# Sparse attention with a mixture of experts: the scale bounds of Q and K taken as sums of magnitudes on ScalarE, the two copies of each high half written by one instruction, and four spreads and the first W2 bounds moved by some steps

## The chip, the core and the metric

The kernel runs on one core of one Trainium2 chip. The metric is the device time of one execution in microseconds (us), median of several runs. Engines are named as in the profile: PE (TensorE, matrix products), DVE (VectorE), ACT (ScalarE), POOL (GpSimd), SP (SyncE, which issues nearly all the DMAs).

## What is computed

Attention over 4 batches, 8 heads, 768 positions and a head size of 64, with a block mask (neighbouring blocks, first and last rows and columns of blocks, three sampled blocks a row). Its output, 3072 rows of 512, goes through a softmax gate that is balanced eight times over rows and columns, and then through 8 experts of width 1024, all of them for every row.

```
scores = scale * np.matmul(q, k.transpose(0, 1, 3, 2))
scores = np.where(mask, scores, -1000000000.0)
attn = np.exp(scores - np.max(scores, axis=-1, keepdims=True))
attn = attn / (np.sum(attn, axis=-1, keepdims=True) + 1e-09)
x = np.matmul(attn, v)          # transposed to (batch*seq, heads*dim)
for e in range(E):
    h = np.maximum(x @ w1[e], 0.0)
    out += P[:, e:e + 1] * (h @ w2[e])
```

## The kernel before

All products are made from pairs of 16-bit numbers. A value in 32 bits is scaled by a power of two, its high half is the scaled value rounded to 16 bits, and its low half is what the rounding left. The scale comes from a bound on the magnitudes. That bound is found per partition, spread over the partitions by a transpose on PE (`spread_qk`, L613, for Q and K; `spread_max`, L110, for everything else), reduced on DVE, clamped, and cut to its power of two (`scale_qk`, L619 to L628).

The attention part goes in steps T = 0 to 191, one for each of 32 heads n and each of 6 columns of 128 keys. A step makes four large products of one score tile for the weights (`weights`, L697 and L700), its exponential on ACT (L705), the low half of the exponential on ACT or DVE in turn (`split_lo`, L714 and L716), and three steps later 18 small products with V (`values`, L731). Ten steps ahead of a head its score tiles are made once for their row maxima alone (`scores`, L664 and L667, with the maximum on DVE, L673), which `lower` (L681, L682, and a transposing DMA) folds into Q.

Q and K are loaded for a pair of heads g at a time (`load_qk`, L588). `peak` (L604) takes the largest magnitude of a loaded 128x768 tile on DVE, once for Q and once for K, at steps 12g - 26 and 12g - 24 (for the second pair both at -14). `spread_qk` and `scale_qk` follow at 12g - 20. For each head, `high_qk` writes the high half with two ACT instructions, once to its place (L641) and once to a second place (L642, the "dup"), since the scores need high times high, low times high and high times low. `low_qk` (L646) makes the low half on DVE, and `turn` (L652) has the halves transposed by a DMA.

The order is written out by hand. `at(T, o, fn, ...)` puts a piece of work at a step and a rank within it (FIRST, TURNS, TOPS, SCORES, VALUES, WEIGHTS, LOWS, LATER, LAST); the pieces are then issued by step and rank, and `in_order` keeps each engine in that order. So an instruction that waits holds up all that stands behind it on its engine. Two spare PSUM banks `u` serve in turn, one for the sums of `values` and the other for all spreads and for `turn_x` (L762), which transposes finished heads on PE and copies them out on ACT (`xf`, L769). `turn_x` stands at steps 12j + 6 and 12j + 10. The spreads of V's bounds stand at steps 42, 90 and 138 (and -6 for the first batch), and that of the first W1 at 142.

At the end the experts' stage begins. The first W2 (2 MB, `load_w(2, 0)`, issued at step 184) is bounded by eight maxima on DVE (L187), two at each of the steps 188 to 191, spread (L110) at 193 and turned into a scale at 194. `stage1` (L1167, L1179) makes the first products of the experts, `stage2` (L1282, L1303) the second. From here on the engines' work is queued by a planner with costs and due times (class `Slots`), which the change does not touch.

Of the kernel before, what the change touches and what calls it, by code (L numbers as in the profile page):

```python
# [14 lines left out]
BF16 = mybir.dt.bfloat16  # L15
AF = mybir.ActivationFunctionType
# [10 lines left out]
EXP_SHIFT = 18.664973875118524  # L27
WALL = 2.0 ** 15
QKTOP = 2.0 ** 9
QKTINY, QKHUGE = 1.0, 2.0 ** 50  # L30
HDOWN = 2.0 ** -20
HUP = 2.0 ** 20
EPS = 1e-9
# [22 lines left out]
def tile_sparse_attention_moe(  # L56
# [338 lines left out]
    with ExitStack() as actx:  # L395
# [202 lines left out]
        def peak(g, m):  # L598
            if m == 0:
                qk[g] = tuple(  # L600
                    col.tile([P, w], F32, tag=f"qk{w}{i}", name=f"qk{i}_{g}")
                    for i, w in enumerate((2, 2, 2, 1))
                )
            nc.vector.tensor_reduce(  # L604
                out=qk[g][0][:, m : m + 1],
                in_=raws[g, m].rearrange("p h c d -> p (h c d)"), axis=AX.X,
                op=ALU.max, apply_absolute_value=True,
            )

        def spread_qk(g):  # L610
# [19 lines left out]
        def parts_qk(n, m):  # L630
            g, j = divmod(n, 2)
            t = (qss[n % NQS], kss[n % NKS])[m]
            if m == 0:
                hi, dup, lo = t[:, 0, :, D:], t[:, 1, :, :D], t[:, 0, :, :D]
            else:
                hi, dup, lo = t[:, 0, :, :D], t[:, 0, :, D:], t[:, 1, :, :D]
            return raws[g, m][:, j], qk[g][2][:, m : m + 1], hi, dup, lo

        def high_qk(n, m):
            src, s, hi, dup, _ = parts_qk(n, m)  # L640
            nc.scalar.activation(hi, src, AF.Copy, scale=s)  # L641
            nc.scalar.activation(dup, src, AF.Copy, scale=s)  # L642

        def low_qk(n, m):
            src, s, hi, _, lo = parts_qk(n, m)
            nc.vector.scalar_tensor_tensor(  # L646
                out=lo, in0=src, scalar=s, in1=hi, op0=ALU.mult, op1=ALU.subtract
            )

        def turn(n, m):  # L650
# [162 lines left out]
        for b in range(B):  # L813
            T0 = b * H * NC
            at(T0 - 30 if b else -17, FIRST, load_v, b)
            for n, T in enumerate((-25, -19, -18, -13) if b else (-13, -13, -11, -9)):
                at(T0 + T, LATER, peak_v, b, n)
            at(T0 - 6, TURNS, scale_spread, f"v{b}")
            at(T0 - 12, LATER, room_v, b)
            at(T0 - 6, LATER, scale_v, b)  # L820
# [13 lines left out]
        def start_w():  # L834
            load_w(1, 0)
            parts, whole, spread, power = scale_steps(1, 0)
            for T, part in zip((101, 106, 107, 113, 118, 119, 125, 130), parts):
                at(T, LATER, part)
            at(130, LATER, whole)
            at(142, TURNS, spread)  # L840
            at(142, LATER, power)

        def start_sums():
            one, two, three, by_p = first_sums()
# [13 lines left out]
        def start_w2():  # L858
            load_w(2, 0)
            parts, whole, spread, power = scale_steps(2, 0)  # L860
            for n, part in enumerate(parts):
                at(188 + n // 2, LATER, part)
            at(NTILE, LATER, whole)
            at(NTILE + 1, LAST, spread)
            at(NTILE + 2, LATER, power)

        at(100, FIRST, start_w)
        at(140, FIRST, start_sums)
# [554 lines left out]
```

## Time and profile before

| | us |
|---|---|
| median of 3 runs | 2336.94 (2335.74 to 2338.75) |
| the profiled execution | 2332.6 |
| its span, first to last instruction | 2330.8 |
| attention, first to last exponential (L705) | 37.0 to 454.2 |
| first product of `stage2` (L1282) | 499.0 |
| PE, DVE, ACT, POOL busy | 94%, 86%, 54%, 55% of the span |

The span is what the profiler saw of one execution; 1.8 us of that execution lie around it. A busy share is a mean over the whole span, and the stages differ. In the tables of windows each row is a stretch of the span with the busy time of each engine and, behind it, the granted clock of PE (1.00 is full). In the tables of waits a row says which engine and line stood still for which other engine and line, for how long in total, how often, and the longest.

### The profile page before, as it was taken

The numbers are of one execution on the slowest core, as the hardware profiler recorded it, in microseconds if no ns is written. First come the engines' busy times: TensorE is split into PE (matmuls) and PEld (weight loads), VectorE is DVE, ScalarE is ACT, GpSimd is POOL, SyncE is SP. The second block draws the span as 40 slices with busy tenths as digits, with TensorE's granted clock in tenths as the row PEclk, the third lists the DMA queues.
The fourth block names the chain that finished last, engine by engine and source line by source line (L and its number), as shares of the span: only waits on it lengthen the run. The fifth ranks groups of instructions, "written<-read, shape, count | busy, mean of one in ns | idle before, by whom it ended". The sixth has DMA issues, their size and how long they took to land.

```text
span 2330.8 us, 47300 instructions
## 1 busy us (share of the span) xinstructions
PE 2192.4 (94%) x18892; PEld 1607.8 (69%) x18892; DVE 1999.7 (86%) x3570; ACT 1255.6 (54%) x2173; POOL 1289.9 (55%) x1235
## 2 busy tenths in 40 slices
PE   5999988889899999999999999999999999999999
PEld 3767666657666677677767776777677767776677
DVE  8999999888789888988898889888988898889876
ACT  4888888665465444444444445444444454445442
POOL 2012334496376665756575657565756575657553
PEclk9999999999999999999999999999999999999999
DMA  6667765413112211221122121212121212121221
GB/s 152 131 123 165 188 128 123 136 62 111 48 49 84 85 49 49 84 84 49 57 75 85 48 74 59 85 48 84 49 84 49 84 48 85 49 84 48 76 75 55
DMA packets 191890, 192.36 MB, mean 83 GB/s; under 512 B 131740, under 2 KB 144052, under 8 KB 191668
## 3 DMA queue, kind: packets, MB, share of 16 engines
q1 hardware_dynamic: 191104, 189.30, 28.2%
q8 instruction: 148, 2.42, 0.4%
q14 instruction: 74, 0.61, 0.1%
q10 hardware_dynamic: 564, 0.03, 0.0%
HBM read 140.54 MB, written 17.30 MB: 68 GB/s over the span
## 4 chain that ended last, share of the span: by engine, by line
PE 48%; DVE 8%; POOL 5%; issue 3%; ACT 2%; DMA 2%; DVEq 0%; POOLq 0%; SPq 0%
PE p L1167 24%; PE py L1282 24%; DVE acc L1303 2%; POOL r L1046 2%; DMA r<-in_moe_w_dram 2%; DVE h L1199 1%; POOL h L1199 1%; DVE a L1179 1%; DVE mx_w L187 1%; ACT h L1189 1%; ACT attic L1031 1%; POOL s L1241 1%; DVE u L1179 1%; DVE attic L1035 1%; DVE w2p L1035 1%
## 5 line engine op out<-in xcount | busy, mean ns | idle before, releaser
L1282 PE MATMUL py<-w2p,h 128*128 128x256 f16 x8064 | 952.3, 273 | 19.6 <-DVE w2p L1035 7.8
L1282 PEld LDWEIGHTS <-h 128*128 128x128 f16 x8064 | 790.8, 98 | 159.7 <-issue 19.1
L1303 DVE SCALAR_TENSOR_TENSOR acc<-py,spare,acc 128x256 f32<-128x256 f32 (+1 forms) x840 | 455.1, 579 | 36.4 <-PE py L1282 35.5
L1199 POOL TENSOR_TENSOR h<-u,h 128x384 f16<-128x384 f32 x128 | 126.7, 990 | 589.8 <-ACT h L1189 589.8
L1167 PEld LDWEIGHTS <-attic 128*128 128x128 f16 x3072 | 304.1, 99 | 215.0 <-issue 40.3
L1167 PE MATMUL p<-attic 128*128 128x384 f16 x2304 | 418.5, 331 | 24.6 <-DVE r L1179 19.4
L1167 PE MATMUL p<-arena 128*128 128x384 f16 x2304 | 409.5, 327 | 16.3 <-DVE arena L1035 11.5
L1167 PEld LDWEIGHTS <-arena 128*128 128x128 f16 x2304 | 225.5, 98 | 150.6 <-DVE arena L1035 13.5
L1189 ACT ACTIVATE h<-c 128x384 f16<-128x384 f32 x256 | 133.6, 522 | 342.5 <-DVE c L1179 272.4
L705 ACT ACTIVATE pe<-t,shift,qk 128x768 int32<-128x768 f32 x192 | 189.9, 990 | 73.7 <-PE t L700 67.8
L1179 DVE SCALAR_TENSOR_TENSOR a<-p,a 128x384 f32<-128x384 f32 x384 | 210.8, 549 | 19.8 <-PE p L1167 15.0
L673 DVE TENSOR_REDUCE top<-m 128x1 f32<-128x768 f32 x192 | 181.6, 948 | 12.6 <-PE m L667 12.3
L1189 ACT ACTIVATE h<-r 128x384 f16<-128x384 f32 x256 | 132.4, 521 | 67.5 <-POOL r L1053 63.2
L1241 POOL TENSOR_TENSOR s<-a,u 128x384 f32<-128x384 f32 x128 | 130.9, 1022 | 49.1 <-ACT a L1238 48.9
L1053 POOL TENSOR_TENSOR r<-s,r 128x384 f32<-128x384 f32 x128 | 149.4, 1167 | 10.0
L1053 POOL TENSOR_TENSOR c<-c,r 128x384 f32<-128x384 f32 x128 | 149.3, 1166 | 10.0
L1046 POOL TENSOR_TENSOR r<-r 128x256 f32<-128x256 f32 (+1 forms) x106 | 135.6, 1304 | 26.6 <-DVE arena L1035 26.6
L1167 PE MATMUL p<-arena,attic 128*128 128x384 f16 x768 | 148.4, 330 | 0.0
L1199 POOL TENSOR_TENSOR h<-c,h 128x384 f16<-128x384 f32 x128 | 143.3, 1120 | 3.5 <-ACT h L1189 3.5
L1179 DVE SCALAR_TENSOR_TENSOR r<-p,a 128x384 f32<-128x384 f32 x128 | 70.5, 551 | 83.4 <-PE p L1167 65.9
L664 PE MATMUL m<-kt,qt 128*128 128x512 f16 (+1 forms) x384 | 128.2, 334 | 14.6 <-DVE top L673 7.3
L1189 ACT ACTIVATE h<-s 128x384 f16<-128x384 f32 x128 | 66.9, 522 | 136.5 <-POOL s L1241 136.3
(206 smaller groups left out, 3731.2 us busy)
## 6 DMA issues: line engine op xcount, KB each, us to landing
arena<-xd SPq DMA_DIRECT2D x128, 384.0 KB, 3.9
attic<-xd SPq DMA_DIRECT2D x96, 384.0 KB, 4.1
r<-in_moe_w_dram SPq DMA_DIRECT2D x16, 2048.0 KB, 8.5
arena<-in_q_dram SPq DMA_DIRECT2D x16, 384.0 KB, 4.2
arena<-in_k_dram SPq DMA_DIRECT2D x16, 384.0 KB, 4.6
arena<-in_v_dram SPq DMA_DIRECT2D x4, 1536.0 KB, 7.6
xd<-xs_t SPq DMA_DIRECT2D x16, 384.0 KB, 4.7
out_dram<-acc SPq DMA_DIRECT2D x24, 256.0 KB, 2.0
```

Of the source, the lines that this page charges most:

```text
L664: nc.tensor.matmul(sc[:, lo:hi], lhsT=qt[:, 0, c], rhs=ka[:, lo:hi], start=True, stop=False)
L673: nc.vector.tensor_reduce(out=tops[n][:, c : c + 1], in_=sc[:, :S], axis=AX.X, op=ALU.max)
L705: nc.scalar.activation(pe, sc[:, :S], AF.Exp, bias=shift, scale=qk[n // 2][3])
L1046: lambda c=c: Pinned.gpsimd.tensor_tensor(out=out[:, c], in0=x[:, c], in1=y[:, c], op=op),
L1053: nc.gpsimd.tensor_tensor(out=out, in0=x, in1=y, op=ALU.subtract)
L1167: nc.tensor.matmul(ps, lhsT=w1p[p][:, l, kc, fs], rhs=xp[p][:, r, kc], start=(kc == 0 and m == 0), stop=(kc == KH - 1 and m == 2),)
L1179: nc.vector.scalar_tensor_tensor(out=t, in0=ps, scalar=HDOWN, in1=other, op0=ALU.mult, op1=ALU.add)
L1189: nc.scalar.activation(h[:, 0], src, AF.Relu if relu else AF.Copy)
L1199: eng.tensor_tensor(out=h[:, 1], in0=src, in1=h[:, 0], op=ALU.subtract)
L1241: nc.gpsimd.tensor_tensor(out=s1, in0=a1, in1=u3, op=ALU.add)
L1282: nc.tensor.matmul(py, lhsT=hs[i, p, kc][:, l, tsl], rhs=w2p[p][:, r, kc], start=(kc == 0 and m == 0), stop=(kc == KF // 2 - 1 and m == 2),)
L1303: nc.vector.scalar_tensor_tensor(out=dst, in0=src, scalar=c, in1=dst, op0=ALU.mult, op1=ALU.add)
```

## The change

The bounds of Q and K are no longer the largest magnitude, found on DVE, but the sum of magnitudes along the row, found by one ACT instruction (`AF.Abs` with an accumulated output; its elementwise result goes to a tile `unread` that nothing reads). A sum is at least as large as the maximum, so it is a bound too; the upper clamp is raised. The two copies of a high half are written by one ACT instruction that reads its source twice through a broadcast; for that, Q's high and low halves change places in the tile. Of the work laid out by hand, the spreads of V's bounds and their scales move from 12j + 6 to 12j + 7, the spread and scale of the first W1 from 142 to 143, the eight maxima of the first W2 from 188 to 191 to 192 and 193, their summary from 192 to 194, the spread from 193 to 194 and the scale from 194 to 195.

```diff
@@ -103,6 +103,11 @@
+    unread = const.tile([P, S], BF16, name="unread")
+
+    def magnitude(engine, total, src):
+        engine.activation(unread[:, : src.shape[1]], src, AF.Abs, accum_out=total)
@@ -601,10 +606,9 @@
-            nc.vector.tensor_reduce(
-                out=qk[g][0][:, m : m + 1],
-                in_=raws[g, m].rearrange("p h c d -> p (h c d)"), axis=AX.X,
-                op=ALU.max, apply_absolute_value=True,
+            magnitude(
+                nc.scalar, qk[g][0][:, m : m + 1],
+                raws[g, m].rearrange("p h c d -> p (h c d)"),
             )
@@ -631,20 +635,20 @@
             if m == 0:
-                hi, dup, lo = t[:, 0, :, D:], t[:, 1, :, :D], t[:, 0, :, :D]
+                hi, lo = t[:, :, :, :D], t[:, 0, :, D:]
             else:
-                hi, dup, lo = t[:, 0, :, :D], t[:, 0, :, D:], t[:, 1, :, :D]
+                hi, lo = t[:, 0].rearrange("p c (two d) -> p two c d", two=2), t[:, 1, :, :D]
...
         def high_qk(n, m):
-            src, s, hi, dup, _ = parts_qk(n, m)
+            src, s, hi, _ = parts_qk(n, m)
+            src = src.unsqueeze(1).to_broadcast([P, 2, NC, D])
             nc.scalar.activation(hi, src, AF.Copy, scale=s)
-            nc.scalar.activation(dup, src, AF.Copy, scale=s)
@@ -815,9 +819,9 @@
-            at(T0 - 6, TURNS, scale_spread, f"v{b}")
+            at(T0 - 5, TURNS, scale_spread, f"v{b}")
...
@@ -859,10 +863,10 @@
             for n, part in enumerate(parts):
-                at(188 + n // 2, LATER, part)
+                at(NTILE + n // 4, LATER, part)
```

In the order of the instructions, a name such as `pe_5_730` is the tile, the step within the head, and a running number; the lines of the new kernel lie 4 or 5 further down. First, ACT around step 11 before: two rows for each high half of Q (`qs`) or K (`ks`).

```order
L714 ACTIVATE pl_3_658<-pe_3_656 128x768
L705 ACTIVATE pe_5_730<-t_5_725,shift,qk_0_181 128x768
L641 ACTIVATE qs_110<-arena,qk_2_340 128x6x64
L642 ACTIVATE qs_110<-arena,qk_2_340 128x6x64
L705 ACTIVATE pe_0_765<-t_0_760,shift,qk_1_232 128x768
L714 ACTIVATE pl_5_732<-pe_5_730 128x768
L705 ACTIVATE pe_1_799<-t_1_794,shift,qk_1_232 128x768
L641 ACTIVATE ks_112<-arena,qk_2_340 128x6x64
L642 ACTIVATE ks_112<-arena,qk_2_340 128x6x64
```

The same place in the new kernel:

```order
L718 ACTIVATE pl_3_649<-pe_3_647 128x768
L109 ACTIVATE unread,qk_3_695<-arena 128x768
L709 ACTIVATE pe_5_721<-t_5_716,shift,qk_0_182 128x768
L646 ACTIVATE qs_111<-arena,qk_2_335 128x12x64
L709 ACTIVATE pe_0_755<-t_0_750,shift,qk_1_229 128x768
L718 ACTIVATE pl_5_723<-pe_5_721 128x768
L109 ACTIVATE unread,qk_3_695<-arena 128x768
L709 ACTIVATE pe_1_789<-t_1_784,shift,qk_1_229 128x768
L646 ACTIVATE ks_113<-arena,qk_2_335 128x2x6x64
```

Each pair of rows for a high half is one row of twice the size, and two rows with the sum of magnitudes (L109) stand ahead of two exponentials; the two L604 rows of a pair of heads are gone from DVE. In the whole program ACT has one row that loads a function table, before and now.

Second, DVE at the end of attention before: the low halves (`pl`) of the last steps between the maxima of the first W2 (`mx_w`), then the first combination of the experts' stage (L1179).

```order
L716 TENSOR_SCALAR pl_1_7840<-pe_1_7838 128x768
L187 TENSOR_REDUCE mx_w_0_7730<-r_0_7728 128x1 x2
L716 TENSOR_SCALAR pl_2_7867<-pe_2_7865 128x768
L187 TENSOR_REDUCE mx_w_0_7730<-r_0_7728 128x1 x2
L716 TENSOR_SCALAR pl_3_7901<-pe_3_7899 128x768
L187 TENSOR_REDUCE mx_w_0_7730<-r_0_7728 128x1 x2
L716 TENSOR_SCALAR pl_4_7934<-pe_4_7932 128x768
L187 TENSOR_REDUCE mx_w_0_7730<-r_0_7728 128x1 x2
L716 TENSOR_SCALAR pl_5_7963<-pe_5_7961 128x768
L1179 SCALAR_TENSOR_TENSOR r_0_0_8130<-p_0_0_8131,a_0_0_8121 128x384
```

The same place in the new kernel:

```order
L720 TENSOR_SCALAR pl_1_7777<-pe_1_7775 128x768
L720 TENSOR_SCALAR pl_2_7804<-pe_2_7802 128x768
L720 TENSOR_SCALAR pl_3_7836<-pe_3_7834 128x768
L720 TENSOR_SCALAR pl_4_7867<-pe_4_7865 128x768
L720 TENSOR_SCALAR pl_5_7894<-pe_5_7892 128x768
L192 TENSOR_REDUCE mx_w_0_7667<-r_0_7665 128x1 x8
L1183 SCALAR_TENSOR_TENSOR r_0_0_8067<-p_0_0_8068,a_0_0_8058 128x384
```

All eight maxima now stand behind the last low half and still ahead of the first combination.

Third, PE around step 42 before: the transposes of a finished head (`xn`), with the spread of V's bound right behind them.

```order
L731 MATMUL u_144<-attic,pe_2_1779 128x66
L762 MATMUL u_145<-ident,xn_2_1556 128x128 x3
L110 MATMUL u_145<-ident,mx_v_1207 128x128
L664 LDWEIGHTS qt_100
L664 MATMUL m_4_1915<-kt_104,qt_100 128x512
```

The spread in the new kernel, one step further:

```order
L735 LDWEIGHTS pe_3_1797
L735 MATMUL u_145<-attic,pe_3_1797 128x66
L115 MATMUL u_146<-ident,mx_v_1193 128x128
L668 LDWEIGHTS qt_101
L668 MATMUL m_5_1928<-kt_105,qt_101 128x512
```

Between `xn` and the spread, which share a bank, there now lies a whole step of products. POOL and SP keep their order.

More of the change, by code (lines that the diff above doesn't have):

```diff
@@ L29 @@
 QKTOP = 2.0 ** 9
-QKTINY, QKHUGE = 1.0, 2.0 ** 50
+QKTINY, QKHUGE = 1.0, 2.0 ** 60
 HDOWN = 2.0 ** -20
@@ L817, in tile_sparse_attention_moe @@
                 at(T0 + T, LATER, peak_v, b, n)
-            at(T0 - 6, TURNS, scale_spread, f"v{b}")
+            at(T0 - 5, TURNS, scale_spread, f"v{b}")
             at(T0 - 12, LATER, room_v, b)
-            at(T0 - 6, LATER, scale_v, b)
+            at(T0 - 5, LATER, scale_v, b)
             for h, hi, lo in ((0, -4, -2), (2, 3, 5), (4, 8, 10), (6, 15, 17)):
@@ L839, in start_w @@
             at(130, LATER, whole)
-            at(142, TURNS, spread)
-            at(142, LATER, power)
+            at(143, TURNS, spread)
+            at(143, LATER, power)
         def start_sums():
@@ L861, in start_w2 @@
             for n, part in enumerate(parts):
-                at(188 + n // 2, LATER, part)
-            at(NTILE, LATER, whole)
-            at(NTILE + 1, LAST, spread)
-            at(NTILE + 2, LATER, power)
+                at(NTILE + n // 4, LATER, part)
+            at(NTILE + 2, LATER, whole)
+            at(NTILE + 2, LAST, spread)
+            at(NTILE + 3, LATER, power)
         at(100, FIRST, start_w)
```

6 lines of the change are left out of this document (3 added, 3 removed).

## The prediction

> **What bounds the kernel now.** First the page, then the busy time of each engine by stretches of the span. Columns: stretch, its length, busy time of PE, PE's weight loads, DVE, ACT, POOL, then PE's granted clock.
>
> ```profile
> 0.00:30.00 30.00, 9.66 (x43) 4.97 (x44) 24.85 (x66) 8.53 (x16) 6.99 (x25) 1.00 0.70 185
> 30.00:90.00 60.00, 55.42 (x648) 36.96 (x648) 55.85 (x106) 43.06 (x57) 8.56 (x13) 0.91 0.66 136
> 90.00:150.00 60.00, 56.92 (x769) 41.02 (x768) 56.83 (x118) 49.22 (x68) 5.64 (x6) 1.00 0.61 114
> 150.00:210.00 60.00, 59.73 (x842) 43.29 (x839) 58.20 (x108) 54.81 (x75) 11.30 (x15) 1.00 0.71 156
> 210.00:270.00 60.00, 53.84 (x729) 38.19 (x726) 54.87 (x100) 48.09 (x66) 21.16 (x25) 0.97 0.70 164
> 270.00:330.00 60.00, 57.22 (x806) 41.35 (x804) 58.94 (x113) 50.74 (x68) 16.56 (x21) 1.00 0.73 154
> 330.00:390.00 60.00, 50.26 (x658) 35.41 (x658) 56.62 (x103) 47.66 (x65) 27.95 (x27) 1.00 0.62 125
> 390.00:450.00 60.00, 51.79 (x791) 38.11 (x789) 54.46 (x76) 50.41 (x64) 30.96 (x26) 1.00 0.61 167
> 510.00:2331.00 1821.00, 1747.11 (x13273) 1296.66 (x13272) 1531.05 (x2708) 868.43 (x1632) 1119.83 (x1045) 0.99 0.20 67
> ```
>
> From 510 us on PE is busy for 1747 of 1821 us, and no instruction there is touched. In attention two engines are nearly full at once: DVE has 91 to 98% of each stretch, PE 84 to 99.6%, and ACT, at 72 to 91%, is third. Which of them sets the pace changes: between 150 and 210 us PE stands still for 0.27 us, between 330 and 390 for 9.74 us.
>
> Then the waits between 30 and 390 us, the stretch in which most of the bounds are taken, and one row of them from 210 to 270 us (the last one).
>
> ```profile
> DVE top L673 <- PE m L667: 9.3, 10, 2.0
> PE u L110 <- ACT xf L769: 7.7, 4, 2.5
> PE m L664 <- DVE top L673: 7.0, 7, 2.2
> PE t L697 <- DVE top L673: 6.2, 9, 2.8
> DVE mx_w L187 <- DMA r<-in_moe_w_dram: 3.0, 1, 3.0
> PE u L613 <- DVE xn L752: 2.1, 4, 0.7
> PE u L762 <- DVE xn L752: 1.8, 2, 1.0
> PE t L697 <- DVE top L673: 3.0, 2, 2.8
> ```
>
> PE waits for DVE for 7.0 + 6.2 + 2.1 + 1.8 = 17.1 us. The longest of these, 2.8 us, lies behind the one wait of DVE for a load (`mx_w`), which stays; 14.3 us are left. A further 7.7 us PE waits in a spread (L110) for ACT to empty the bank (`xf`).
>
> **Part by part: the bounds leave DVE.** By groups, between 30 and 390 us, first the group of DVE and then groups of ACT:
>
> ```profile
> L604 DVE TENSOR_REDUCE qk<-arena 128x1 f32<-128x768 f32 x28 | 26.3, 939 | 0.0
> L705 ACT ACTIVATE pe<-t,shift,qk 128x768 int32<-128x768 f32 x162 | 160.3, 990 | 59.9 <-PE t L700 54.3
> L641 ACT ACTIVATE qs<-arena,qk 128x384 f16<-128x384 f32 x27 | 16.3, 604 | 1.0 <-DVE qk L626 1.0
> L284 ACT ACTIVATE xs_b<-xf 128x768 f16<-128x768 f32 x10 | 8.3, 832 | 0.0
> ```
>
> DVE loses 28 of the 32 maxima here, of 939 ns each, 26.3 us or 4.4 us in 60; the other four lie before 30 us. The end of the stretch can gain from that only what PE waits for DVE, so 14.3 us is the upper end. The lower end is 0: ACT becomes late in DVE's stead. I take 9 us, about 60%, because PE itself is the next to be late. It is busy for 59.73 of 60 us in one stretch, where the 4.4 us bring nothing, and DVE in turn waits 9.3 us for PE, so a part of what DVE gains it waits away.
>
> ACT takes on 28 sums. No instruction of before accumulates on ACT. Without that, one over 128x768 takes 832 ns (L284) or 990 ns (L705, with operands for scale and bias); if the accumulator were read in a second pass it would be twice the latter, 1.98 us. I take 0.9 us, near the two rows: 25 us.
>
> The merged copies go the other way. Two of 604 ns become one of twice the size. From 384 elements (604) and the same with 768 (832 without, 990 with two operands), I take 0.92 us for it, and the bounds are 0.83 and 2 x 0.604 = 1.21. There are four such groups of 27 (Q and K, first and second copy; one is shown), so 54 pairs: 54 x (1.21 - 0.92) = 15.7 us less. So ACT goes from 293.6 us (the sum of its six rows) to about 303 of then some 345 us, 88%. That is below the 91% which it has between 150 and 210 us, and the extra work is hidden behind the exponentials' own waits for PE (54.3 us). If that cover is gone, each sum costs its 0.9 us. A sum stands four steps or more ahead of the spread that needs it, about 8 us at 2.2 us a step, which is the 417 us of this row over 191 steps:
>
> ```profile
> L705 ACT ACTIVATE pe<-t,shift,qk x192: 976/992/997, 37.0 to 454.2; 128x768 int32<-128x768 f32 x192
> ```
>
> So no engine waits for a sum, save at the start.
>
> **The spreads a step later.** The four waits of 7.7 us are, by their place behind `xn`, the V spreads of three batches and the first W1. Each stands right behind `xn` in the same bank, so that PE holds all products until ACT has come round to `xf`. One step of about 2 us, with its products, now lies between; of waits of at most 2.5 us half a microsecond is left at most. I take 5 us, since only what PE's standstill passes on to DVE (`top` waiting for `m`, 9.3 us) is lost to both; the ends are 0 and 7.7. V's scale comes a step later, and POOL, which makes the high halves at 12j + 8, may start on them later. `values` uses them at 12j + 15, eight steps or some 17 us behind the scale; W1's scale has four steps to its first use at 147. So I set the delay at nothing, and at its own step (2 us) if that cover is gone.
>
> **The start.** Operations of before at the start (start and length in us):
>
> ```profile
> 4.37 1.28 ACT L641 ACT_TABLE_LOAD   x1 [4.37 <-DMA arena<-in_q_dram]
> 6.66 1.80 DVE L604 TENSOR_REDUCE qk<-arena 128x1 f32<-128x768 f32 x2
> 9.04 0.42 DVE L621 TENSOR_REDUCE qk<-u 128x2 f32<-128x256 f32 x1 [0.57 <-PE u L613]
> ```
>
> DVE came to the first two maxima only at 6.66, behind the mask's work, and ended them at 8.46. ACT is free when its table is in, at 5.65, and ends two sums of 0.9 us at 7.45: 1.0 us earlier, for all that follows. The ends are a loss of 1.1 us (two sums of 1.98 us would end at 9.61) and a gain of 1.2 (two of 0.83).
>
> **The end of attention.** DVE, ACT and, in the last two rows, all engines in two stretches:
>
> ```profile
> 446.53 0.55 DVE L716 TENSOR_SCALAR pl<-pe 128x768 f16<-128x768 uint16 x1
> 450.34 1.28 DVE L187 TENSOR_REDUCE mx_w<-r 128x1 f32<-128x512 f32 x2 [3.26 <-DMA r<-in_moe_w_dram]
> 451.53 0.55 DVE L716 TENSOR_SCALAR pl<-pe 128x768 f16<-128x768 uint16 x1
> ...
> 456.50 0.55 DVE L716 TENSOR_SCALAR pl<-pe 128x768 f16<-128x768 uint16 x1
> 458.60 0.56 DVE L1179 SCALAR_TENSOR_TENSOR r<-p,a 128x384 f32<-128x384 f32 x1 [1.55 <-ACT a L1214]
> ...
> 459.51 0.56 DVE L1179 SCALAR_TENSOR_TENSOR a<-p,a 128x384 f32<-128x384 f32 x1 [0.29 <-PE p L1167]
> 460.49 0.56 DVE L1179 SCALAR_TENSOR_TENSOR u<-p,a 128x384 f32<-128x384 f32 x1 [0.42 <-PE p L1167]
> ```
> ```profile
> 448.54 0.99 ACT L705 ACTIVATE pe<-t,shift,qk 128x768 int32<-128x768 f32 x1 [0.25 <-PE t L700]
> 454.20 0.99 ACT L705 ACTIVATE pe<-t,shift,qk 128x768 int32<-128x768 f32 x1 [4.67 <-PE t L700]
> ```
> ```profile
> 450.00:454.00 4.00, 1.86 (x15) 1.17 (x16) 3.66 (x7) 0.00 (x0) 0.00 (x0) 0.58 0.14 56
> 454.00:458.00 4.00, 4.00 (x38) 2.73 (x37) 3.05 (x6) 1.45 (x2) 0.00 (x0) 0.57 0.02 4
> ```
>
> DVE waits 3.26 us for the W2 load with finished exponentials behind it. The low half that PE needs comes at 451.53, so PE is idle for half of four microseconds, then runs at a granted clock of 0.57, and ACT waits 4.67 us for the last score tile. In the new order the low halves go ahead: the next at about 447.0, the last exponential at 449.5 (right behind the one of 448.54) and its low half by 451.5. Then the eight maxima, 8 x 0.64 = 5.1 us, to 456.6; the load is there by then (450.34). The first combination starts at 456.6 in place of 458.60. In the next two combinations DVE waited 0.29 + 0.42 = 0.7 us for PE; now PE makes their products while the maxima run. That gives 2.0 + 0.7 = 2.7 us. The W2 scale moves with it and is used only by the splitting of W2, whose first product (`stage2`) starts at 499.0 in the table above; the products of `stage1` up to there cover it. The spread of W2 now stands on PE ahead of the last `xn`, which comes later by that one small transpose.
>
> The lower end is 0, if POOL's sums or the late parts of x take it back. For the upper end, PE has 1.86 + 4.00 = 5.9 us of work in the eight microseconds at a granted clock of 0.575; at full clock 2.5 us less, so 2.7 + 2.5 = 5.2 us. The Trainium skill, "TensorE: Matmul & The Clock Gate", section "Part 1: The HAM clock gate", says that the clock halves after an idle window of some 3.4 us and comes back only after as long a busy one. The trace agrees in kind: the clock is still at 0.57 in the second row, where PE is busy throughout. By that rule, with PE's standstill gone, the term would be the 5.2 and the sum 20.2 in place of 17.7. I keep 2.7, because in the new order the maxima on DVE end last and not PE.
>
> **The sum.** 1.0 + 9 + 5 + 2.7 = 17.7 us. The profiled execution, 2332.6 us with 1.8 outside the span, would be at about 2315; the median of before lies 4.3 above that execution, at 2336.94, and I take the same difference off it: **2319 us**.
>
> **The rivals.**
> *All of PE's waits go.* DVE no longer paces attention at all, and PE runs through: 1.2 + 14.3 + 7.7 + 5.2 = 28.4 us, 2308.5. For it: more DVE work goes (26.3 us) than PE waits (14.3). Against it: the stretches where PE is already full, and the ones from 390 us on, in which no bound is taken. Chance 0.15.
>
> *ScalarE holds up what DVE gives free.* A sum stands directly ahead of two exponentials in twelve steps, and these come 0.9 us later; low halves and `values` follow them. Then the 9 us are 0, the spreads give half and the end 2: 1 + 0 + 2.5 + 2 = 5.5, 2331. For it: ACT at 91% in the densest stretch. Against it: three steps between an exponential and its use. Chance 0.15.
>
> *Slower: the function table is swapped.* If the sum of magnitudes needs another table than the exponential, ACT loads one before and one after each sum. The trace has one load in all:
>
> ```profile
> L641 ACT ACT_TABLE_LOAD  x1: 1283/1283/1283, 4.4 to 4.4; - x1
> ```
>
> 28 x 2 x 1.28 = 72 us more: ACT would have 303 + 72 = 375 us of work for a stretch of 360. At the 97% that DVE reaches at most over 60 us (58.20), the stretch takes 387 us, 27 more than now, and with some 4 us back at start and end the time is 2336.9 + 27 - 4 = 2360. It decides from where ACT has 0.97 x 360 = 349 us of work: 46 us over the 303, or 1.6 us more for each sum. A very dear accumulator would come to the same. Against it: exponential and copy share a table now, and the written order has one load, as before. By the Trainium skill, "ScalarE: Activation LUTs", section "Table sets: the hidden batching unit", the magnitude function lies in the set of the exponential, as a filler of every set, so no swap would come. The same page, "What ACT_TABLE_LOAD costs", gives about 2.66 us for a swap with its drain, twice the price used here; no run here shows either. Chance 0.04.
>
> **Chances and range.** The forecast has 0.62 (gains of 11 to 25 us), the first two rivals 0.15 each, the third 0.04; 0.04 is for none of these. A range of 2308 to 2331.5 takes in the first two, and with them the upper ends of all four terms; what it leaves out is the third, the unnamed, and the case in which every term is at its lower end (no gain), about one in eight in all. A measurement of this kernel tells a difference of about 0.2%, 4.7 us, from none. Faster by more than that: 0.62 + 0.15 + two thirds of 0.15 = 0.87; within: the rest of that and some of the unnamed, 0.08; slower: 0.05.
>
> **What would show it.** Right: DVE's 26 us of bounds gone, sums on ACT near 0.9 us and merged copies near 0.92; no wait of L110's spread for `xf` beyond half a microsecond; PE's waits for `top` between 30 and 390 us down by about 60%; no wait of DVE for the W2 load, the first L1179 about 17 us earlier than 458.6, and the stage from there to the end as long as before. Wrong: more than one table load; sums above 2 us; new waits of PE for `pe`; or the first product of `stage2` less than 10 us earlier.

## The result, and the profile after

| | before | after | the same changed kernel, timed again (e7) |
|---|---|---|---|
| median, us | 2337.85 (first set), 2336.21 (e7's set) | 2311.48 | 2315.81 |
| ratio to before, 95% interval | | 0.9892 [0.9868, 0.9917] | 0.9916 [0.9903, 0.9930] |
| profiled execution, us | 2332.6 | 2309.9 | 2319.4 |
| its span, us | 2330.8 | 2308.1 | 2317.5 |
| first exponential | 37.0 | 34.7 | 34.7 |
| exponential of step 180 | 432.1 | 418.6 | 421.1 |
| first product of `stage2` | 499.0 | 483.6 | 484.0 |
| from there to the end of the span | 1831.8 | 1824.5 | 1833.5 |

The change makes the kernel faster, by 25.2 us in the first set (19.4 to 30.8, from the interval times 2337.85) and by 19.6 in the second (16.4 to 22.7). Both hold together between 19.4 and 22.7, so about 20 us is the figure to explain. By the profiles, 15.4 and 15.0 us of it lie ahead of the first product of `stage2`. The 7.3 us by which the stage behind it is shorter in the first profile are not the change's: in e7, the very same program, that stage takes 1.7 us more than before. Over the profiles of all kernels here it takes 1824.5 to 1834.2 us, and none of them changes an instruction there. (What the clock has to do with that spread is in the last section.)

First the busy time by stretches in the changed kernel, columns as in the prediction: stretch, length, PE, weight loads, DVE, ACT, POOL, granted clock.

```profile
30.00:90.00 60.00, 58.16 (x694) 39.24 (x694) 54.09 (x106) 49.12 (x63) 7.82 (x13) 0.91 0.65 139
90.00:150.00 60.00, 59.13 (x804) 42.81 (x803) 55.62 (x116) 53.10 (x69) 5.63 (x6) 1.00 0.63 125
150.00:210.00 60.00, 58.94 (x846) 42.71 (x845) 53.70 (x100) 55.78 (x75) 12.27 (x17) 1.00 0.68 149
210.00:270.00 60.00, 55.96 (x736) 40.15 (x734) 55.26 (x104) 51.63 (x68) 24.15 (x24) 0.97 0.78 173
...
330.00:390.00 60.00, 53.07 (x728) 37.85 (x726) 57.78 (x97) 51.51 (x68) 29.33 (x27) 1.00 0.54 120
```

PE is fuller: 58.16 of 60 us between 30 and 90 (55.42 before), 59.13 between 90 and 150 (56.92). DVE is down by 1.2 to 4.5 us in the first three rows, and ACT reaches 55.78 of 60. A stretch holds more steps than before, so a row is not the same work; the next two are, from the first exponential to that of step 180, first of before, then of after.

```profile
37.00:432.10 395.10, 366.54 (x4975) 261.74 (x4975) 374.65 (x687) 328.72 (x439) 106.23 (x114) 0.99 0.66 142
```
```profile
34.70:418.60 383.90, 364.81 (x4974) 261.58 (x4974) 356.60 (x660) 338.95 (x436) 107.40 (x116) 0.99 0.67 146
```

The same 4974 or 4975 products take PE 365 to 367 us in both. What shrinks is the time in which PE stands still, from 395.10 - 366.54 = 28.6 us to 19.1. DVE is relieved of 18.1 us, and ACT has 10.2 us more.

These are PE's and DVE's waits in the changed kernel between 30 and 380 us, about the steps that 30 to 390 held before (engine, line and what it waits for: total, times, longest).

```profile
DVE top L677 <- PE m L671: 15.9, 25, 1.7
PE t L701 <- DVE top L677: 11.2, 13, 2.4
PE m L668 <- DVE top L677: 3.1, 3, 1.9
DVE mx_w L192 <- DMA r<-in_moe_w_dram: 3.0, 1, 3.0
PE u L766 <- DVE xn L756: 2.5, 4, 0.8
```

The spreads' wait for `xf`, 7.7 us before, is gone. PE's waits for `top` are not: 14.3 us here, 13.2 before. The waits that did fall are those for `xn` (2.5 us; 3.9 before). DVE in turn waits 15.9 us for PE, where it waited 9.3.

Most of the waits for `top` stand behind work of DVE that the change leaves alone, which goes some way to explain why they stay. From the first exponential to step 180 PE waits 13.6 us for `top` in the kernel before. Only 2.5 us of that come where a maximum of Q or K started on DVE within the 4.5 us (two steps) ahead of the late `top`; with 6 us it is 4.1. The rest follows `lower`, the low halves of V, the scale chains of Q and K, and the maxima of W1. Of the 3.9 us of waits for `xn`, 1.9 have such a maximum within 4.5 us. One late `top` behind `lower` (L682, now L686), with the product that waits for it, before and then after:

```profile
423.21 1.20 DVE L682 SCALAR_TENSOR_TENSOR qs<-top,qs 128x6 f16<-128x6 f32 x1
424.31 0.94 DVE L673 TENSOR_REDUCE top<-m 128x1 f32<-128x768 f32 x1
...
425.31 0.38 PE L697 MATMUL t<-qt,kt 128*128 128x512 f16 x1 [1.70 <-DVE top L673]
```
```profile
409.73 1.20 DVE L686 SCALAR_TENSOR_TENSOR qs<-top,qs 128x6 f16<-128x6 f32 x1
410.83 0.94 DVE L677 TENSOR_REDUCE top<-m 128x1 f32<-128x768 f32 x1
...
411.82 0.38 PE L701 MATMUL t<-qt,kt 128*128 128x512 f16 x1 [1.69 <-DVE top L677]
```

What the changed instructions cost, by line (duration in ns, least, median and most; first and last start):

```profile
L109 ACT ACTIVATE unread<-arena x32: 827/836/842, 4.4 to 366.7; 128x768 bf16<-128x768 f32 x32
L109 ACT ACTIVATION_READ_ACCUMULATOR unread<-arena x32: 185/192/199, 5.1 to 367.4; 128x1 f32 x32
L109 ACT ACT_TABLE_LOAD  x1: 1283/1283/1283, 2.0 to 2.0; - x1
```
```profile
L646 ACT ACTIVATE qs<-arena,qk x32: 922/927/937, 9.0 to 390.7; 128x768 f16<-128x768 f32 x32
```

A sum is two instructions, 836 and 192 ns, and overlaps itself a little: at the start the pair begins at 4.39 and ends at 5.32, 0.93 us, against the 0.9 assumed. A merged copy takes 0.927 us (0.92 assumed). There is one table load in the whole program, now ahead of the first sum.

The start of the changed kernel (start and length, in us):

```profile
2.03 1.28 ACT L109 ACT_TABLE_LOAD   x1 [2.03 <-issue]
4.39 0.84 ACT L109 ACTIVATE unread<-arena 128x768 bf16<-128x768 f32 x1 [1.08 <-DMA arena<-in_q_dram]
5.14 0.18 ACT L109 ACTIVATION_READ_ACCUMULATOR unread<-arena 128x1 f32 x1
7.16 0.42 DVE L625 TENSOR_REDUCE qk<-u 128x2 f32<-128x256 f32 x1 [0.41 <-PE u L617]
```

The table is loaded while Q is still on its way, so the first sum starts with Q's landing, at 4.39, and the reduction that stood at 9.04 stands at 7.16.

At the end of attention, two views: ACT's last exponential, and DVE.

```profile
437.38 0.99 ACT L709 ACTIVATE pe<-t,shift,qk 128x768 int32<-128x768 f32 x1 [0.21 <-PE t L704]
```
```profile
438.41 0.56 DVE L720 TENSOR_SCALAR pl<-pe 128x768 f16<-128x768 uint16 x1 [0.64 <-ACT pe L709]
438.88 4.83 DVE L192 TENSOR_REDUCE mx_w<-r 128x1 f32<-128x512 f32 x8
443.63 0.55 DVE L1183 SCALAR_TENSOR_TENSOR r<-p,a 128x384 f32<-128x384 f32 x1
```

The last exponential waits 0.21 us for its tile, not 4.67. The eight maxima of W2 follow the last low half without a wait for the load, and the first combination follows them at once, at 443.63 (458.60 before).

### The profile page after: what moved, and what is told of

The parts are those of the page before. It is cut to its first block, busy times and chain, and to the rows that moved or that the text cites. A ratio compares the mean times of both kernels' runs of the same rounds, so it can differ in the third digit from the quotient of the medians.

```text
span 2308.1 us, 47281 instructions
## 1 busy us (share of the span) xinstructions
PE 2178.5 (94%) x18892; PEld 1602.8 (69%) x18892; DVE 1980.7 (86%) x3538; ACT 1269.1 (55%) x2173; POOL 1287.1 (56%) x1235
## 4 chain that ended last, share of the span: by engine, by line
PE 49%; DVE 8%; POOL 5%; issue 3%; ACT 2%; DMA 2%; DVEq 0%; POOLq 0%; SPq 0%
PE py L1286 25%; PE p L1171 25%; DMA r<-in_moe_w_dram 2%; DVE acc L1307 2%; POOL r L1050 2%; DVE h L1203 1%; POOL h L1203 1%; DVE a L1183 1%; ACT h L1193 1%; DVE mx_w L192 1%; ACT attic L1035 1%; POOL r L1057 1%; DVE w2p L1039 1%; POOL a L1057 1%; POOL s L1245 1%
## 5 line engine op out<-in xcount | busy, mean ns | idle before, releaser
L1171 PE MATMUL p<-attic 128*128 128x384 f16 x2304 | 411.1, 327 | 27.8 <-DVE r L1183 19.2
L1183 DVE SCALAR_TENSOR_TENSOR a<-p,a 128x384 f32<-128x384 f32 x384 | 211.2, 550 | 18.9 <-PE p L1171 13.6
L1203 DVE TENSOR_TENSOR h<-s,h 128x384 f16<-128x384 f32 x128 | 110.1, 860 | 37.2 <-ACT h L1193 37.0
L701 PE MATMUL t<-qt,kt 128*128 128x512 f16 (+1 forms) x384 | 127.0, 331 | 14.0 <-DVE top L677 13.8
```

The lines of the kernel that those rows point to most:

```text
L701: nc.tensor.matmul(sc[:, lo:hi], lhsT=kt[:, 0, c], rhs=qa[:, lo:hi], start=True, stop=False)
L1171: nc.tensor.matmul(ps, lhsT=w1p[p][:, l, kc, fs], rhs=xp[p][:, r, kc], start=(kc == 0 and m == 0), stop=(kc == KH - 1 and m == 2),)
L1183: nc.vector.scalar_tensor_tensor(out=t, in0=ps, scalar=HDOWN, in1=other, op0=ALU.mult, op1=ALU.add)
L1203: eng.tensor_tensor(out=h[:, 1], in0=src, in1=h[:, 0], op=ALU.subtract)
```

## The experiments

Each part of the change was put into the kernel before by itself, then in pairs and triples. A is the sums on ACT, B the merged copies, C the spreads a step later, D the W2 bounds at the end of attention. Times are medians; each ratio is to the kernel before on the same chip.

| | us | ratio, 95% interval | difference, us | first exponential to step 180 | first product of `stage2` |
|---|---|---|---|---|---|
| before (profile of the page) | 2336.94 | | | 395.1 | 499.0 |
| A (e1) | 2326.80 | 0.9967 [0.9955, 0.9979] | -7.7 | 393.5 | 495.4 |
| B (e2) | 2333.30 | 0.9994 [0.9984, 1.0005] | -1.4 | 396.3 | 500.2 |
| C (e3) | 2327.59 | 0.9976 [0.9962, 0.9989] | -5.6 | 391.9 | 495.7 |
| D (e4) | 2331.64 | 0.9986 [0.9975, 0.9998] | -3.3 | 399.9 | 502.3 |
| A, C (e9) | 2323.68 | 0.9946 [0.9934, 0.9959] | -12.6 | 386.5 | 488.3 |
| B, C, D (e5) | 2323.61 | 0.9947 [0.9932, 0.9961] | -12.4 | 392.4 | 492.7 |
| A, C, D (e10) | 2318.56 | 0.9921 [0.9906, 0.9936] | -18.5 | 386.3 | 484.0 |
| all (e7) | 2315.81 | 0.9916 [0.9903, 0.9930] | -19.6 | 386.4 | 484.0 |

The four single differences add up to 18.0 us, and the whole has 19.6: in time, the parts add up, within these intervals. One profile of attention can be off by some us, as D's row shows: that kernel is faster by its times and 3.3 us later at `stage2` in its one profile. The mean granted clock from the first exponential to step 180 also differs among the profiles, from 0.978 (e11) and 0.981 (D) to 1.000 (e12); by estimate 0.01 of some 385 us is about 4 us. Where the two differ, the times decide.

**A alone: the sums (e1).** The upper clamp is raised too.

```diff
...
+    unread = const.tile([P, S], BF16, name="unread")
+    def magnitude(engine, total, src):
+        engine.activation(unread[:, : src.shape[1]], src, AF.Abs, accum_out=total)
...
-            nc.vector.tensor_reduce(
...
+            magnitude(
```

> Only the bounds move from DVE to ACT; two copies, all spreads and the W2 maxima as before. Measure: start of the first product of stage2 (499.0 us before, 483.6 with the whole change), and the length from there to the end (1831.8 and 1824.5). If DVE's freed time is what attention gains from: first product of stage2 at 488 to 492 (1 to 2.3 us at the start, 6 to 9 us behind it). If ACT's queue holds it up without the merged copies: 496 or later. The rest of the span: if the 7.3 us there come from PE's clock and differ by run, anything from 1824 to 1833; if the new tile shifts addresses and so speeds the experts' stage, near 1824.5.

Measured: 7.7 us faster. The profile has 3.6 of them ahead of `stage2`, 2.3 at the start and 1.3 behind it, and none later; the rest is not located, since that profiled run, 2329.8, lay 3.0 above the kernel's own median, and that of before 4.3 below. Here are the waits of this kernel between 30 and 386 us:

```profile
DVE top L677 <- PE m L671: 21.4, 24, 2.5
PE t L701 <- DVE top L677: 9.9, 13, 1.8
PE u L115 <- ACT xf L773: 7.1, 4, 1.8
PE m L668 <- DVE top L677: 3.9, 3, 2.2
...
PE u L766 <- DVE xn L756: 0.7, 1, 0.7
```

DVE's gain shows as DVE's own waiting, 21.4 us for PE. PE waits as long for `top` as before (13.8 us), and the spreads hold it up as before (7.1). What fell is PE's wait for `xn`, to 0.7 us from 3.9. The first product of `stage2`, at 495.4, came later than the 488 to 492 that I had put it at, and just short of the 496 of the other case. So DVE's relief brings less in the steps than forecast (7.7 us less the start's 2.3 is 5.4, against 9), and not by the waits that were to give it.

**C alone, and A with C (e3, e9).** e3 moves these three places and no other; e9 is e1 and e3 together.

```diff
-            at(T0 - 6, TURNS, scale_spread, f"v{b}")
+            at(T0 - 5, TURNS, scale_spread, f"v{b}")
...
-            at(T0 - 6, LATER, scale_v, b)
+            at(T0 - 5, LATER, scale_v, b)
...
-            at(142, TURNS, spread)
-            at(142, LATER, power)
+            at(143, TURNS, spread)
+            at(143, LATER, power)
```

> Only the spreads of V and of the first W1 move by a step. Theory: PE's four waits of 7.7 us for the bank go, and 3 to 5 us of them reach the end of attention: first product of stage2 at 494 to 496. Rival, DVE paces those steps alone: waits gone, but 498 to 499.5.

> Only the sums on ACT and the moved spreads of V and W1; two copies, and the W2 maxima as before. If the parts add up: exponential of step 180 at 424 to 425 (3.9 + 3.8 us). If they help each other, because the freed time is waited away at the spreads when these stay: 419 to 421. Time: 0.57% below before if additive, 0.75% or more if not.

Measured: C gains 5.6 us, A and C together 12.6, about their sum of 13.3. Step 180 of e9 came at 421.3, where it was put if the two help each other (419 to 421), but the time of 0.54% is that of parts that add. PE's waits from the first exponential to step 180, first of C alone (36.4 to 428.3 us), then of A with C (34.8 to 421.3 us):

```profile
PE t L697 <- DVE top L673: 9.6, 11, 2.5
PE u L762 <- DVE xn L752: 3.4, 4, 1.0
PE u L613 <- DVE xn L752: 2.9, 4, 1.2
...
PE m L664 <- DVE top L673: 2.2, 5, 0.6
...
PE u L110 <- ACT xf L769: 0.6, 1, 0.6
```
```profile
PE t L701 <- DVE top L677: 13.2, 16, 1.8
PE u L766 <- DVE xn L756: 2.3, 3, 0.8
...
PE m L668 <- DVE top L677: 1.1, 2, 0.9
```

With C the wait for `xf` goes from 7.7 to 0.6, and the next late thing is `xn` on DVE: 3.4 + 2.9 = 6.3 us, where the kernel before had 3.9. With the maxima off DVE, that falls to 2.3. The waits for `top` do not fall, both rows together grow from 11.8 to 14.3. So the sums pay where PE waits for the finished head, and not at the row maxima.

**B alone, and all but B (e2, e10).** In e2 only the high halves are merged; e10 is the changed kernel with the two separate copies of before.

```diff
...
 def high_qk(n, m):
-            src, s, hi, dup, _ = parts_qk(n, m)
+            src, s, hi, _ = parts_qk(n, m)
+            src = src.unsqueeze(1).to_broadcast([P, 2, NC, D])
             nc.scalar.activation(hi, src, AF.Copy, scale=s)
-            nc.scalar.activation(dup, src, AF.Copy, scale=s)
```

> Only the two copies of a high half become one instruction. If ACT has slack: first product of stage2 at 498 to 499.5, no change of time (within 3 us). If ACT is late in attention and its 15 us of relief count: 496 or earlier, 3 us or more faster.

> The whole change but for the merged copies: each high half is again written by two instructions (some 18 us more on ACT, 64 x 0.28). The sums made twice had cost 15 us of time for 33 us on ACT. If ACT stands at the margin once it makes the sums: exponential of step 180 at 424 to 430 us (418.6 and 421.1 in two profiles of the whole change), time 4 to 10 us above the whole change. If the copies bring here what they bring alone (0.06%): step 180 at 422 or earlier, time within 3 us.

Measured: B alone is not told from nothing (the interval holds 1). Taken out of the whole, no cost can be told either: 0.9921 and 0.9916 have intervals that overlap nearly whole. ACT's busy time from the first exponential to step 180 is 346.42 us of 386.30 in e10, 90%, against 338.95 of 383.90:

```profile
34.70:421.00 386.30, 363.86 (x4974) 260.78 (x4974) 357.77 (x660) 346.42 (x493) 107.56 (x116) 0.99 0.66 145
```

The merged copies' 7.5 us are room on ACT from which no gain can be told here.

**D alone (e4).**

```diff
-                at(188 + n // 2, LATER, part)
-            at(NTILE, LATER, whole)
-            at(NTILE + 1, LAST, spread)
-            at(NTILE + 2, LATER, power)
+                at(NTILE + n // 4, LATER, part)
+            at(NTILE + 2, LATER, whole)
+            at(NTILE + 2, LAST, spread)
+            at(NTILE + 3, LATER, power)
```

> Only the maxima, spread and scale of the first W2 move. Theory: last low half and first combination come 2.5 to 4.5 us earlier and it stays so: first product of stage2 at 494.5 to 496.5. Rival, POOL's sums or the late parts of x take it back: first combination earlier, but first product of stage2 at 498 or later.

Measured: 3.3 us faster, the interval from 0.5 to 5.8. The profile's first product of `stage2` is late, at 502.3, because that execution had lost time in attention, ahead of anything that D touches. From the exponential of step 186 to that product it takes 52.8 us, where before took 56.2, A alone 56.6 and C alone 56.8. The kernels with D have 51.8 to 53.0 there, those without it 54.5 to 56.8. So D gives about 3 us.

**All but A (e5).** The changed kernel with the maximum on DVE kept, and its old upper clamp.

```diff
-            magnitude(
...
+            nc.vector.tensor_reduce(
...
+                op=ALU.max, apply_absolute_value=True,
```

> The whole change but for the sums: bounds of Q and K stay maxima on DVE. Measure in the profile: exponential of step 180 (432.1 us before, 418.6 with the whole change, 428.2 with the sums alone, 428.3 with the spreads alone). If the parts add up: 428, and a time about 8 us above the whole change (the sums alone gave 0.33%). If the sums are worth more once the spreads no longer hold PE: 428 too, but 10 us or more above the whole change; so it is the next kernel, sums and spreads alone, that tells the two apart together with this one.

Measured: 12.4 us faster than before, so the sums are worth 12.4 to 19.6, that is 7.2 us, with the rest in place. The two single profiles have more, 392.4 - 386.4 = 6.0 us up to step 180 and 1.7 at the start. Alone A had 7.7 by its times: the two agree.

**The changed kernel unaltered (e7)** was run beside these.

> The changed kernel once more, unaltered, for more runs of it. If the 7.3 us that the experts' stage was shorter in its first profile come from a chance of that run: the part from the first product of stage2 on takes 1824 to 1833 us here, and the median is 2312 to 2320. If they belong to the kernel: 1824 to 1826, median 2309 to 2313.

Its numbers stand in the tables above: the gain is there again, and the short experts' stage of the first profile is not.

**Each sum twice, and no sum at all (e6, e11).** If ACT's work were what holds up the changed kernel, twice the sums would cost, and none would gain.

```diff
     def magnitude(engine, total, src):
         engine.activation(unread[:, : src.shape[1]], src, AF.Abs, accum_out=total)
+        engine.activation(unread[:, : src.shape[1]], src, AF.Abs, accum_out=total)
```

> The whole change with each sum of magnitudes made twice on ACT: 32 more of about 1.0 us (an elementwise pass of 0.84 and the read of the accumulator, 0.19). The output is the same. If ACT has the slack that the prediction gave it: exponential of step 180 within 3 us of 418.6, start 1 to 2 us later, time within 4 us of the whole change. If ACT is the next to be late: step 180 later by 8 to 30 us.

e11 leaves out the finding of the bounds: a fixed 300.0 stands in their place.

```diff
+        level = aconst.tile([P, 2], F32, name="level")
+        nc.vector.memset(level, 300.0)
...
-            magnitude(
...
+                qk[g] = (level,) + qk[g][1:]
```

> The whole change with no bound found at all: Q and K take a fixed one (300, near the sums of these data), and ACT makes no sums; spreads and scales stay. What it leaves out is the finding of the bounds. If ACT's 33 us of sums cost time at the rate at which doubling them did: step 180 at 403 to 413, time 8 to 16 us below the whole change. If PE and the PSUM buffers are next to be late: within 4 us of the whole change.

Measured: e6 2331.11 us, 0.9980 [0.9971, 0.9989], 15.3 us above e7. e11 2310.84, 0.9900 [0.9885, 0.9916]: by the ratios 3.7 us below all of the change, with intervals that overlap. That is less than the 8 to 16 us which e6's rate would give, and not told from none. In attention its profile gains nothing, with the first product of `stage2` at 485.1 (484.0 in e7), but its granted clock there is 0.978 against 0.986 in e7, which by estimate hides some 3 us. The stretch from the first exponential to step 180, of e6 and of e11:

```profile
35.50:436.40 400.90, 369.40 (x4976) 261.55 (x4976) 359.64 (x660) 362.07 (x491) 109.80 (x116) 0.99 0.64 140
```
```profile
34.70:421.50 386.80, 367.36 (x4976) 263.18 (x4976) 356.39 (x659) 321.99 (x383) 106.75 (x116) 0.98 0.67 145
```

ACT does 322 us in e11, 339 in the changed kernel, 346 in e10, and the stretch stays at 384 to 387 us. At 362, in e6, it is 400.9. The sums, then, cost a few us on ACT at most, with room for some 7.5 us more and not for 23. And new waits appear in e6 (35.5 to 436.4 us):

```profile
DVE pl L721 <- ACT pe L710: 11.2, 13, 1.7
PE u L736 <- ACT pl L719: 4.6, 10, 0.7
```

DVE waits 11.2 us for exponentials and PE 4.6 for low halves of ACT; between 30 and 386 us the changed kernel has 0.4 of the first. The rival in which ScalarE holds up what DVE gives free is real, one more 0.9 us for each sum away. Whether it is ACT's total or the block of 2 us straight ahead of an exponential, these runs don't tell.

**The next wait (e8).** In the changed kernel DVE waits 3.0 us for the first W1 load. This kernel is the changed one with the first maximum over that load four steps later.

```diff
-            for T, part in zip((101, 106, 107, 113, 118, 119, 125, 130), parts):
+            for T, part in zip((105, 106, 107, 113, 118, 119, 125, 130), parts):
```

> The whole change with the first of the eight maxima of the first W1 moved from step 101 to step 105, so that DVE does not stand for its load (3.0 us, with PE idle and its clock halved behind it). If that standstill reaches the end: steps 102 to 108 take about 13 us in place of 17.7, and the time is 3 to 5 us below the whole change. If DVE makes it up elsewhere: within 2 us.

Measured: 2310.65 us, 0.9896 [0.9882, 0.9911]. The two rows are that maximum, in e7 and in e8:

```profile
245.85 0.69 DVE L192 TENSOR_REDUCE mx_w<-r 128x1 f32<-128x512 f32 x1 [3.07 <-DMA r<-in_moe_w_dram]
```
```profile
250.62 0.68 DVE L192 TENSOR_REDUCE mx_w<-r 128x1 f32<-128x512 f32 x1
```

The wait is gone, the steps 96 to 108 take 26.1 us (29.5 after, 30.9 in e7), those from 102 on 13.7 of them (about 13 expected), and the first product of `stage2` comes at 478.0. By the times the gain on e7 is 0.9916 against 0.9896, some 5 us; the intervals touch, so it is likely and not proven. At the same mean granted clock of 0.990 e8 took 2309.7 and 2310.1 us, e7 2315.5 to 2319.4, on different chips. It is the earliest `stage2` of all kernels here.

**DVE loaded again (e12).** e8, with a third of the low halves on ACT in place of a half, the others on DVE.

```diff
-PLAN = 'da'
+PLAN = 'dda'
```

> As the kernel with the first W1 maximum moved, and in addition ACT makes a third of the low halves of the exponentials up to step 178 and not half of them: some 29 fewer of 0.83 us on ACT, as many more of 0.59 us on DVE. If ACT is the late engine after the change: 4 to 10 us below the kernel with the moved maximum alone. If DVE is then late in its stead: within 3 us of it, or slower.

Measured: 2323.22 us, 0.9948 [0.9935, 0.9961], 12.6 us slower than e8. The stretch from the first exponential to step 180:

```profile
34.40:424.40 390.00, 363.11 (x4975) 260.66 (x4975) 374.27 (x690) 319.38 (x407) 109.73 (x116) 1.00 0.66 144
```

DVE is back at 374.27 us, as busy as in the kernel before (374.65). ACT has the least to do of all, and it does not help. So DVE's load still decides in the changed kernel, though PE's waits for `top` never moved much (15.3 us here, 13.7 in e8; those for `xn` are 4.5 and 2.5).

## Why the prediction was right, and where its reasons were not

Forecast 2319 us, 17.7 us below the median before; measured 2311.48 and 2315.81, or 19.6 to 25.2 us less. Both times lie in the range. Point by point:

- **The start, 1.0 us forecast, 2.3 measured.** The term was mis-sized in one assumption: that the table load stays behind Q's arrival, to 5.65 us. In the changed kernel it waits for nothing and is in by 3.31. The first sum starts at 4.39, when Q has landed. By the reduction (9.04 to 7.16) that gives 1.9 us; where the other 0.4 up to the first exponential come from is not located.
- **The bounds off DVE, 9 us forecast with part of it at 60% of PE's waits.** Measured -7.7 alone and -7.2 with the rest, the start's 2.3 (1.7 against e5) in it, so 5.4 or 5.5 us in the steps: between the ends 0 and 14.3, below the value taken. The failed step is "PE's waits for `top` between 30 and 390 us down by about 60%". They stayed (13.2 and 14.3 us), and few of them stood close behind a maximum of Q or K: 2.5 of 13.6 us, and 1.9 of 3.9 for `xn`, 4.4 together. That is the likely reason, read from the order of DVE's rows; no run moved the other work, and in C, where 1.5 of the 6.3 us for `xn` have such a maximum close ahead, 4.0 fell. The relief itself was mis-sized as well. Only 18.1 us went from DVE's busy time, because neighbouring rows of DVE overlap: the 27 maxima of this stretch are 25.4 us long by their rows, but by the trace DVE's busy time without them would be only some 21 us less. In C against A with C, what fell was PE's wait for `xn`, 6.3 to 2.3, and DVE's own wait for PE, 10.5 us up to step 180 before, is 16.9 to 22.6 in the kernels with A, save e12 (9.1). The step priced the relief by the waits with the largest totals, without asking what DVE did ahead of each.
- **ACT takes the sums without cost.** Right to within some 4 us: without any sum (e11) no gain is told from none. The margin was too wide. The prediction let ACT become late from 1.6 us more for each sum, and e6 loses 15.3 us to about 0.9 us more for each; e10 bounds the margin from the other side.
- **Merged copies, nothing forecast.** Right: -1.4 us alone, not told from 0, and no loss told without them. Their room on ACT was not needed to cover the sums, though 0.927 us for the instruction was met.
- **The spreads, 5 us forecast, 5.6 measured.** Right in size and place: 7.7 us of waits became 0.6 in C alone, and none is left in the whole. A part came back as waits for `xn`, 3.9 to 6.3.
- **The end, 2.7 us forecast, 3.3 measured (0.5 to 5.8).** The order of events was as written: no wait for W2, the exponentials close together, the maxima last, the combination behind them. They took 4.83 us (5.1 assumed), and the first combination came 15.0 us earlier (17 forecast). The 5.2 us that full clock and no standstill would have given are inside the interval too, so it does not choose between the two sums; the 3.4 us from step 186 to `stage2` in e4 (56.2 - 52.8) lie nearer to the 2.7. In the first profile of the changed kernel PE is busy throughout and its clock is at 0.99 to 1.00 from 430 to 442 us, so full clock and no standstill were there, and the term still stayed near the 2.7.
- **The experts' stage as long as before.** Right within its scatter, 1824.5 to 1834.2 us.
- **The rivals.** All of PE's waits gone: no, 19.1 us of standstill remain up to step 180. ScalarE late: not in this kernel, but in e6. A table swap: no, one load in 32 sums among 192 exponentials. The Trainium skill, "ScalarE: Activation LUTs", section "Table sets: the hidden batching unit", says that the magnitude function lies in every set as a filler; the trace agrees. The price of the swap was a little high: it takes 58.20 us as the most that DVE has in 60, but the table above it has 58.94 (270 to 330 us), which makes 22 us in place of 27, and 2355 in place of 2360.
- **What carried it.** The sum of the forecast terms, 1.0 + 9 + 5 + 2.7, stands beside 2.3 + 5.4 + 5.6 + 3.3 = 16.6 measured part by part, or 18.0 with B's -1.4. Too little at the start was made up in part by too much in the steps, so that the total came this close is partly luck. Some of the 19.6 to 25.2 us may be the clock's (last section).

## What to carry to other kernels

When two engines are nearly full in turn, work taken off one of them brings less than the waits for it add up to, and not at the waits that looked largest: for each wait, look what the late engine did just ahead of it, since a wait that stands behind work which stays need not fall. Look also which short wait comes next (here `xn`), and expect part of the relief as idle time of the relieved engine. Test each part alone and each part taken out of the whole; where the times of the parts add up, one profile that says otherwise can be scatter, and its granted clock is the first thing to look at. Before work is moved to an engine off the critical path, measure its room by doing the moved work twice, and by leaving it out.

## What the runs showed of the hardware

An accumulated activation is followed by an instruction of its own that reads the accumulator, 185 to 199 ns, so that a sum over 768 columns costs 0.93 us and not 0.84. The load of the function table stood behind Q's landing in one kernel (4.37) and behind nothing in the other (2.03); why it differs, the trace doesn't show.

TensorE's clock explains part of the experts' scatter. The mean granted clock of that stage is 0.998 in the first profile of the changed kernel and 0.995 in e10, the two shortest (1824.5 and 1825.4 us). In the other twelve profiles, 1826.6 to 1834.2 us, it is 0.989 to 0.993. The times go with the clock too. Of 35 runs of the kernel before on one chip, the three with a mean of 0.991 or 0.992 take 2327.7 to 2330.2 us, the four with 0.983 or 0.985 take 2336.9 to 2341.3. At 0.989 and 0.990 there are 13 runs of the kernel before with a median of 2332.7 us, and five of the changed one with a median of 2316.0. So of the 20 us to explain some 3 may be the clock's. Whether the change itself brings a fuller clock, these runs don't tell.

When the clock falls can be read from the traces. In each of the 14 it changes only at whole multiples of 3.41 us from its first recorded change. Here is the same standstill of 2.46 us in the experts' stage, before and then after, as the product that ends it, with the idle time in brackets:

```profile
1003.00 0.32 PE L1167 MATMUL p<-attic 128*128 128x384 f16 x1 [2.46 <-DVE r L1179]
```
```profile
988.07 0.32 PE L1171 MATMUL p<-attic 128*128 128x384 f16 x1 [2.46 <-DVE r L1183]
```

And the windows of that grid around it, again before and then after:

```profile
1000.20:1003.61 3.41, 0.95 (x8) 0.54 (x6) 3.30 (x4) 2.16 (x4) 3.05 (x3) 0.99 0.00 0
1003.61:1007.02 3.41, 3.41 (x14) 1.76 (x12) 3.31 (x8) 1.60 (x4) 0.00 (x0) 0.51 0.00 0
```
```profile
983.05:986.47 3.42, 2.56 (x21) 1.89 (x20) 3.42 (x5) 2.12 (x4) 3.34 (x4) 1.00 0.00 0
986.47:989.88 3.41, 1.81 (x12) 1.10 (x12) 3.19 (x6) 1.45 (x3) 1.84 (x1) 1.00 0.00 0
989.88:993.29 3.41, 3.41 (x32) 3.01 (x31) 3.31 (x7) 2.27 (x5) 0.20 (x1) 1.00 0.00 0
```

Before, the standstill lies within one window, in which PE is busy for 0.95 us, and the next window has half the clock: 14 products in 3.41 us. After, it lies across the border of two, with 2.56 and 1.81 us of work, and the clock stays full: 32 products. Over the windows at full clock of all 14 traces, 122 have less than 1.4 us of PE's busy time, and each is followed by one at half; of 8918 with more than 1.7 us, 8915 are followed by one at full clock; of the 159 between, 42 by one at half. So a gap's length does not decide alone: what counts is how much work is left in one window, and so where the gap falls.

The Trainium skill, "TensorE: Matmul & The Clock Gate", section "Part 1: The HAM clock gate", has a window of some 3.4 us that runs free, and halves the clock after an idle one. The traces agree on the window (3.41 us), but an idle one need not be without work: 0.95 us of it did not keep the clock full.
